# The last four attention units of a fused top-k attention and gated network take the path of all others

## The chip, the cores and the metric

The kernel runs on one core of one Trainium2 chip. The metric is the device time of one execution in microseconds, the median of three runs. Engines are called PE or TensorE (matmuls), DVE or VectorE, ACT or ScalarE, POOL or GpSimd, and SP or SyncE, whose queue here only issues DMAs.

## The reference, cut to what matters

Attention with 8 batches, 8 heads, 576 tokens and a head of 64 elements keeps the 32 largest scores of each row; its result, laid out as 4608 tokens by 512, goes through a network with a cosine gate.

```python
scores = scale * np.matmul(q, k.transpose(0, 1, 3, 2))
kth = np.partition(scores, -top_k, axis=-1)[..., -top_k:-top_k + 1]
scores = np.where(scores >= kth, scores, -1000000000.0)
scores = scores - np.max(scores, axis=-1, keepdims=True)
attn = np.exp(scores)
attn = attn / (np.sum(attn, axis=-1, keepdims=True) + 1e-09)
attn_out = np.matmul(attn, v)
x = attn_out.transpose(0, 2, 1, 3).reshape(B * S, H * D)      # 4608 x 512
h = x @ w_in                                                   # 4608 x 2048
out = (h * np.cos(h)) @ w_out                                  # 4608 x 512
```

## The kernel before, in words

**Units and blocks.** The 4608 tokens are cut into 36 blocks of 128. A *unit* is one block and one pair of heads, so there are 144 units, four per block (`NU` = 144). A block's network part starts when the attention of its four units has been written, transposed, into the tile `xT`.

**One unit of attention.** `scores` makes two 128 x 576 score matrices in PSUM (448 columns in a tile of tag `sc`, which has two buffers, the last 128 in the tile `rim`). `take_scores` copies them to `s` in SBUF on ScalarE. The search for the 32nd largest runs on VectorE in rounds of "eight largest" (MAX8) and "replace these" (MATCH_REPLACE8). A *folded* search works on 288 columns: `fold_high` makes the larger of the two halves of a row, `fold_sum` and `fold_low` on GpSimd the smaller (sum less larger, on the bits), four rounds search the larger, two the smaller, and `merge_first`, `merge_second` find the threshold in the two sorted lists. `bounds` and `distances` turn it into two biases, `mask` and `exponentials` (ScalarE) into weights with their sums, `sums` and `reciprocal` (VectorE) into 1/denominator.

**Two ways to transpose the weights.** Units 0 to 139 go through memory: `split` (GpSimd) separates the 16-bit halves of the weights and of the reciprocal into the tile `halves` (one buffer), `write_halves` writes them to memory, and `transposes` reads them back with a transposing DMA into `pT` (three buffers), both from SP's queue. `values` multiplies with v on TensorE, into `rim`, for two units at once; `take_values` multiplies by the transposed reciprocal on VectorE into `xT`. The last four units, 140 to 143, instead have `normalise` multiply the weights by the reciprocal on GpSimd, `transposes_now` transpose them as nine blocks of 128 x 128 on TensorE, into a tile of tag `sc` and `rim`, with three ScalarE copies to `pT`, and `values` and `take_values` (a ScalarE copy) follow in the same slot for that one unit. Units 142 and 143 are also searched without folding, on 576 columns.

**The network.** `ff1` is one call of the first product (two 128-column groups of h for one block; eight calls a block), `ff2` one of the second (two of 16 terms of the sum; eight calls a block). The first product's result lies in one of two PSUM banks (tag `mm`, also used by the second product's sum); `take_first` (ScalarE) evicts it twice, as h/2pi and as a rounded integer; `reduce_first` and `reduce_second` subtract them; `sines` (ScalarE) takes the cosine; `gate` multiplies; `ff2` reads that. `take_second` evicts the sum and sends it out. Reductions and gate run on GpSimd, and on VectorE once `ff["end"]` is set, as it is from slot 144 on.

**The order of the work.** The schedule is written out by hand: every engine runs its instructions in the order in which the program issues them. Slot `i` (`slot`) searches unit `i`, masks and takes exponentials of unit `i - 1`, sends unit `i - 2` to memory, and in even slots multiplies the pair `i - 4`, `i - 3` with v. `scored` says which slot makes which unit's scores; some slots make two. `feed(n)` puts up to `n` calls of `ff1` or `ff2` into TensorE's order, by credit (5 per slot less 0.9 per unit of scores), by `can_first` and `can_second` (are the inputs a few ticks old?) and by an alternation of two and two (`ff["kind"]`, `ff["half"]`). `open_bank` first evicts what is full when both banks are taken. Slots 141 to 144 are `last_slot`. A loop then forwards what is left of the network.

Of the launch, only the order of the slots matters here. The functions that the diff touches:

Of the kernel before, what the change touches and what calls it, by code (L numbers as in the profile page):

```python
# [10 lines left out]
F32 = mybir.dt.float32  # L11
# [6 lines left out]
P = 128  # L18
TOPK = 32
# [11 lines left out]
def kernel(  # L31
# [202 lines left out]
    def take_scores(u):  # L234
        s = u["s"] = work.tile([P, 2, S], F32, tag="s", name="s", bufs=4)
        nc.scalar.copy(out=s[:, :, 0:SB], in_=u["sc"][:, :, 0:SB])  # L236
        nc.scalar.copy(out=s[:, :, SB:S], in_=sc_ends[u["n"] % 2])  # L237
        if not u["folds"]:
            del u["sc"]

    def fold_high(u):

# [15 lines left out]

    def fold_sum(u):

        if not u["folds"]:
            return
        s = u["s"].bitcast(I32)
        u["low"] = work.tile([P, 2, HS], F32, tag="low", name="low", bufs=1)
        nc.gpsimd.tensor_tensor(  # L265
            out=u["low"].bitcast(I32), in0=s[:, :, 0:HS], in1=s[:, :, HS:S], op=ALU.add
        )

    def fold_low(u):

        if not u["folds"] or u["n"] in BUSY:
            return
        low = u["low"].bitcast(I32)
        nc.gpsimd.tensor_tensor(  # L274
            out=low, in0=low, in1=u["rest"][:, :, HS:S].bitcast(I32), op=ALU.subtract
        )
# [15 lines left out]
    def topk_first(u, w):  # L292

        u["top"] = tops[u["n"] % len(tops)]
        merges = w and w["folds"]
        if merges:
            merge_first(w)
        if u["folds"]:
            if u["n"] not in BUSY:
                fold_sum(u)  # L300
            fold_high(u)
        else:
            u["rest"] = work.tile([P, 2, S], F32, tag="rest", name="rest", bufs=1)
        if merges:
            merge_second(w)
        if u["folds"] and u["n"] in BUSY:
            fold_now(u)
        topk_round(u, 0, [lambda: bounds(w), lambda: distances(w)] if w else ())

    def topk_round(u, rnd, between=(), ahead=None):  # L310
        top, rest, lasts = u["top"], u["rest"], TOPK // 8 - 1
        end = TOPK - 1 - 8 * rnd
        at = top[:, :, end : end - 8 if rnd < lasts else None : -1, 0]
        if u["folds"]:
            search(
                at, rest[:, :, HS:S] if rnd == 0 else rest[:, :, 0:HS], rest[:, :, 0:HS], rnd < lasts,
                between if rnd < lasts else (),
            )
        else:
            search(at, u["s"] if rnd == 0 else rest, rest, rnd < lasts, between)  # L320
        if rnd < lasts:
            return
        del u["rest"]
        if u["folds"]:
            low = u.pop("low")
            for k in range(TOPK // 16):
                more = k < TOPK // 16 - 1
                if ahead and not more:
                    take_values(ahead)
                search(  # L330
                    top[:, :, 1 + 8 * k : 9 + 8 * k, 1], low, low, more,
                    () if more or rnd < lasts else between,
                )

# [22 lines left out]
    def bounds(u):  # L359

        top = u.pop("top").rearrange("p j r i -> p j (r i)")
        end = 2 * TOPK
        if not u["folds"]:
            nc.vector.tensor_copy(out=top[:, :, end - 1], in_=top[:, :, 0])
        less = u["less"] = top[:, :, end : end + 2]
        u["near"] = top[:, :, end - 1 : end + 1]
        nc.vector.tensor_reduce(
            out=less, in_=top[:, :, end - 2 : end].unsqueeze(3), axis=mybir.AxisListType.X,
            op=ALU.max, negate=True,
        )  # L370
# [35 lines left out]
    def both(u):  # L406
        return [lambda: sums(u), lambda: reciprocal(u)] if u else ()

    def normalise(u):
        s, rden = u["s"], u.pop("rden")  # L410
        for j in range(2):
            nc.gpsimd.tensor_scalar(
                out=s[:, j], in0=s[:, j], scalar1=rden[:, j : j + 1], scalar2=1.0,
                op0=ALU.mult, op1=ALU.mult,
            )

    def split(u):


# [14 lines left out]
    def transposes(u):  # L436
# [3 lines left out]
        nc.sync.dma_start_transpose(  # L440
            out=words.rearrange("p (c q) -> p c q", c=2 * NT + 2), in_=rows
        )

    def transposes_now(u):

        s = u.pop("s").rearrange("p j k -> p (j k)")
        tp = ps.tile([P, 2, 512], F32, tag="sc", name="tp", bufs=2)
        for c in range(2 * NT + 1):
            j, k = divmod(c, NT + 1)
            to = room[1][:, 0:P] if c == NT else tp[:, j, k * P : (k + 1) * P]  # L450
            nc.tensor.transpose(to, s[:, c * P : (c + 1) * P], ident)
        pT = u["pT"] = work.tile([P, 2 * NT + 2, P], F32, tag="pT", name="pT", bufs=3)
        for j in range(2):
            at = j * (NT + 1)
            nc.scalar.copy(
                out=pT[:, at : at + NT].rearrange("p c q -> p (c q)"), in_=tp[:, j]
            )
        nc.scalar.copy(out=pT[:, NT], in_=room[1][:, 0:P])

    def values(us):  # L460

# [17 lines left out]
    def take_values(us):  # L479
        blk, hp, n = block_of[us[0]["tok"]], us[0]["hp"], len(us)  # L480
        if "xT" not in blk:
            blk["xT"] = work.tile([P, NP, P], F32, tag="xT", name="xT", bufs=5)
        for i, u in enumerate(us):
            to, o, pT = blk["xT"][:, hp + i], room[0][:, i * P : (i + 1) * P], u.pop("pT")
            if u["paired"]:
                nc.vector.tensor_tensor(out=to, in0=o, in1=pT[:, 2 * NT + 1], op=ALU.mult)
            else:
                nc.scalar.copy(out=to, in_=o)
        blk["left"] -= n
        blk["tick"] = ff["tick"]  # L490

# [154 lines left out]
    def feed(n):  # L646

        ff["tick"] += 1
        while n > 0 and ff["credit"] >= 1:
            for kind in (ff["kind"], 1 - ff["kind"]):  # L650
                if (can_first, can_second)[kind]():
                    break
            else:
                return
# [14 lines left out]

    LAST = NU - NP
    scored, last, last_values = {}, {}, {}
    for i, u in enumerate(units):
        two = i % 2 == 0 and 2 < i < LAST + 2 and (len(u["parts"]) == 1 or u["hp"] == 0)
        scored.setdefault(i - 2 if two else i - 1, []).append(u)
        for part in u["parts"]:
            last[part[0], u["hp"]] = i - 2 if two else i - 1
            last_values[part[0], u["hp"]] = i
# [19 lines left out]

    for i, u in enumerate(units):  # L700
        u["n"] = i
        u["folds"] = i < LAST + 2
        u["paired"] = i < LAST

    def send(x):

# [4 lines left out]
    def slot(i, u, w, x, z):  # L711
# [37 lines left out]
        take_banks()  # L749
        if w and late:  # L750
            exponentials(w)
        take_scores(units[i + 1])
        if w and not late:
            exponentials(w)
        topk_round(u, 3, both(w), z)
# [8 lines left out]
        reduce_first()  # L764
        reduce_second()
        feed(1 if len(made) == 2 else 3)
        if i == LAST:
            sines(1)

    def last_slot(i, u, w, x, z):  # L770
        ff["late"] = False
        if u:
            topk_first(u, w)
            fold_low(u)
            topk_round(u, 1)
        else:
            bounds(w)
            distances(w)
        mask(w)
        exponentials(w)  # L780
        take_banks()
        sines(1)
        if z:
            values(z)
        if i + 1 < NU:
            scores(units[i + 1])
        if z:
            take_values(z)
        if i + 1 < NU:
            take_scores(units[i + 1])  # L790
        if x:
            send(x)
        if u:
            topk_round(u, 2, both(w))
            topk_round(u, 3)
        else:
            sums(w)
            reciprocal(w)
        normalise(w)
        gate(2)  # L800
        feed(2)
        transposes_now(w)
        take_banks()
        reduce_first()
        reduce_second()
        feed(1)
        values([w])
        take_values([w])
        feed(2)

    tt = ps.tile([P, 512], F32, tag="mm", name="warm", bufs=2)
    for _ in range(12):
# [4 lines left out]
    scores(units[0])  # L817
    take_scores(units[0])
    decode_first(3)
    for i in range(NU + 1):  # L820
        ff["end"] = i >= NU
        ff["credit"] = min(ff["credit"] + 5.0 - 0.9 * len(scored.get(i, [])), 5.3)
        ff["now"] += 1
        wq["ready"] = wq["done"]
        u, w = (units[i - n] if 0 <= i - n < NU else None for n in range(2))
        x = units[i - 2] if 0 <= i - 2 < LAST else None
        z = units[i - 4 : i - 2] if i % 2 == 0 and 0 <= i - 4 < LAST else None
        if i <= LAST:
            slot(i, u, w, x, z)
        else:  # L830
            last_slot(i, u, w, x, z)
    while first or second or full:
        ff["now"] += 1
        ff["credit"] = 2.0
        take_banks()
        gate(2)
        reduce_first()
        reduce_second()
        sines(1)
        gate(2)  # L840
        feed(2)


# [35 lines left out]
```

## Time and profile before

| What | us |
|---|---|
| median of three runs | 1461.11 |
| the three runs | 1461.11, 1459.79, 1464.31 |
| profiled execution, its own time | 1461.65 |
| profiled execution, span of the trace | 1459.9 |

| Engine | busy us | share of the span |
|---|---|---|
| TensorE, matmul | 1386.9 | 95% |
| VectorE | 1363.8 | 93% |
| GpSimd | 1157.5 | 79% |
| ScalarE | 1088.2 | 75% |

A line of the timeline gives the start, the busy time (neighbours of one form are merged), the engine, the line of the kernel, the operation, what it writes and reads with the shapes, and how many instructions. A bracket at the end is the idle time of the engine before it, and what ended it. Ends of matmuls are modelled, so the distance from one start to the next is the better measure of what they cost. Buffer numbers are left out of names. A span begins and ends with the traced instructions; the device time of the same execution is 1.75 us longer.

### The profile page before, as it was taken

How to read it: one execution, taken by the hardware profiler on the slowest of the kernel's cores; microseconds unless marked ns; L12 is line 12 of the kernel's file. 1: busy time of each engine (PE TensorE's matmuls, PEld its weight loads, DVE VectorE, ACT ScalarE, POOL GpSimd, SP SyncE). 2: the span in 40 equal slices, each digit the busy share in tenths (PEclk: the TensorE clock that was granted, in tenths of full speed). 3: DMA queues.
4: the chain of work that ended last, by engine and by line, in shares of the span. 5: the costliest groups of instructions: out<-in, count | busy, mean ns of one | idle time of the engine just before them, and what ended most of it. 6: DMA issues, size and time to landing. Idle time of an engine off the chain costs nothing.

```text
span 1459.9 us, 30230 instructions
## 1 busy us (share of the span) xinstructions
PE 1386.9 (95%) x10288; PEld 996.8 (68%) x10288; DVE 1363.8 (93%) x5213; ACT 1088.2 (75%) x1910; POOL 1157.5 (79%) x812
## 2 busy tenths in 40 slices
PE   4387899999999999999999999999999999999998
PEld 2265667777777767777777776777777777777665
DVE  7999999999999999999999999999999999999821
ACT  5787767877777777778777777777777787877641
POOL 5867878888888888888888887888888888888410
PEclk6598999999999999999999999999999999999999
DMA  8986687666665576657655666657665566655300
GB/s 254 282 235 192 175 183 182 155 161 190 179 159 152 168 180 169 161 144 201 185 168 143 144 180 182 170 149 185 192 169 144 152 171 168 166 152 152 62 8 15
DMA packets 427434, 240.00 MB, mean 164 GB/s; under 512 B 375952, under 2 KB 392592, under 8 KB 427280
## 3 DMA queue, kind: packets, MB, share of 16 engines
q1 hardware_dynamic: 418704, 216.88, 57.0%
q10 hardware_dynamic: 8576, 21.19, 4.1%
q8 instruction: 81, 1.33, 0.4%
q14 instruction: 73, 0.60, 0.1%
HBM read 45.09 MB, written 101.19 MB: 100 GB/s over the span
## 4 chain that ended last, share of the span: by engine, by line
PE 82%; DVE 8%; ACT 4%; DMA 3%; POOL 1%; issue 1%; SPq 1%; ACTq 0%; POOLq 0%
PE mm L537 31%; PE o L612 31%; PE rim L477 10%; PE sc L226 7%; DVE top L352 4%; DVE rest L357 2%; PE rim L226 2%; DMA v<-in_v_dram 1%; ACT s L391 1%; ACT s L383 1%; DMA k<-in_k_dram 1%; ACT L391 1%; DMA st<-in_moe_w_in_dram 1%; DVE rest L247 1%; DVE low L357 0%
## 5 line engine op out<-in xcount | busy, mean ns | idle before, releaser
L537 PEld LDWEIGHTS mm<-xT,w_in 128*128 128x128 f32 x4608 | 537.0, 192 | 74.8 <-issue 64.7
L612 PE MATMUL o<-w_out,g 128*128 128x512 f32 x1152 | 538.1, 600 | 12.0 <-POOL w_out L154 7.7
L537 PE MATMUL mm<-xT,w_in 128*128 128x128 f32 x4608 | 540.1, 275 | 6.8 <-ACT x L553 3.9
L352 DVE MAX8 top<-rest 128x8 f32<-128x288 f32 x1148 | 480.7, 454 | 0.0
L424 POOL COPY halves<-s 128x2304 uint16<-128x2304 uint16 x140 | 294.8, 2105 | 149.5 <-ACT s L391 149.1
L357 DVE MATCH_REPLACE8 rest<-top,rest 128x288 f32<-128x288 f32 (+1 forms) x860 | 377.0, 446 | 0.0
L612 PEld LDWEIGHTS o<-w_out,g 128*128 128x128 f32 x1152 | 202.4, 190 | 199.0 <-issue 184.2
L352 DVE MAX8 top<-low 128x8 f32<-128x288 f32 x568 | 240.0, 448 | 0.1
L391 ACT ACTIVATE s<-s,nd 128x576 f32<-128x576 f32 x288 | 220.2, 767 | 0.8
L383 ACT ACTIVATE s<-s,top 128x576 f32<-128x576 f32 x288 | 206.1, 766 | 0.0
L274 POOL TENSOR_TENSOR low<-low,rest 128x576 int32<-128x576 int32 x137 | 193.6, 1413 | 10.7
L265 POOL TENSOR_TENSOR low<-s 128x576 int32<-128x576 int32 x137 | 193.7, 1414 | 6.1 <-ACT s L237 4.9
L226 PE MATMUL sc<-k,q 64*128 64x448 f32 (+1 forms) x640 | 157.9, 591 | 36.8 <-DMA k<-in_k_dram 14.9
L551 ACT ACTIVATE g<-mm 128x512 f32<-128x512 f32 x144 | 85.8, 596 | 128.8 <-PE mm L537 124.6
L582 POOL TENSOR_TENSOR x<-g,x 128x1024 f32<-128x1024 f32 x68 | 160.9, 2366 | 5.7
L477 PE MATMUL rim<-pT,v 128*64 128x128 f32 (+1 forms) x2560 | 159.5, 269 | 2.8 <-DMA pT<-rows 2.8
L599 POOL TENSOR_TENSOR g<-g,x 128x1024 f32<-128x1024 f32 x68 | 161.0, 2367 | 1.3 <-ACT x L592 1.3
L477 PEld LDWEIGHTS rim<-pT,v 128*64 128x64 f32 x2560 | 132.8, 139 | 13.1 <-issue 4.0
L236 ACT COPY s<-sc 128x896 f32<-128x896 f32 x144 | 129.2, 897 | 3.9 <-PE sc L226 3.4
L237 ACT COPY s<-rim 128x256 f32<-128x256 f32 x144 | 55.1, 382 | 91.9 <-PE rim L477 91.9
L357 DVE MATCH_REPLACE8 low<-top,low 128x288 f32<-128x288 f32 x284 | 123.6, 443 | 0.0
L226 PEld LDWEIGHTS sc<-k,q 64*128 64x128 f32 (+1 forms) x640 | 47.5, 183 | 100.2 <-DVE rest L357 47.0
(59 smaller groups left out, 1335.8 us busy)
## 6 DMA issues: line engine op xcount, KB each, us to landing
rows<-halves SPq DMA_DIRECT2D x140, 640.0 KB, 3.0
out_dram<-ob ACTq DMA_DIRECT2D x36, 256.0 KB, 2.4
q<-in_q_dram SPq DMA_DIRECT2D x31, 288.0 KB, 3.9
v<-in_v_dram SPq DMA_DIRECT2D x32, 256.0 KB, 3.4
st<-in_moe_w_out_dram ACTq DMA_DIRECT2D x16, 512.0 KB, 5.1
st<-in_moe_w_in_dram SPq DMA_DIRECT2D x10, 512.0 KB, 6.9
k<-in_k_dram SPq DMA_DIRECT2D x31, 144.0 KB, 3.8
k<-in_k_dram SPq DMA_DIRECT2D x32, 128.0 KB, 3.8
```

Source lines behind the costliest of these rows:

```text
L226: nc.tensor.matmul(to[r0 : r0 + rows, j, 0 : k1 - k0], st["q"][d, q0 : q0 + rows], st["k"][d, k0:k1], start=True, stop=True,)
L265: nc.gpsimd.tensor_tensor(out=u["low"].bitcast(I32), in0=s[:, :, 0:HS], in1=s[:, :, HS:S], op=ALU.add)
L274: nc.gpsimd.tensor_tensor(out=low, in0=low, in1=u["rest"][:, :, HS:S].bitcast(I32), op=ALU.subtract)
L352: nc.vector.max(to[:, j], src[:, j])
L357: nc.vector.match_replace(rest[:, j], to[:, j], src[:, j], NEG)
L383: nc.scalar.activation(out=s[:, j], in_=s[:, j], func=AF.Prelu, bias=less[:, j, 1:2], scale=1.0, alpha=FAR)
L391: nc.scalar.activation(out=s[:, j], in_=s[:, j], func=AF.Exp, bias=nd[:, j : j + 1], scale=SCALE, accum_out=den[:, j, 0:1],)
L424: nc.gpsimd.tensor_copy(out=halves[:, :, 0 : 2 * S], in_=s.rearrange("p (k h) -> p h k", h=2))
L477: nc.tensor.matmul(o[d, to], lhsT, rhs, start=c == 0, stop=c == NT)
L537: nc.tensor.matmul(mm[:, at : at + w], w_in[f // FC][:, c, (f % FC) * P : (f % FC + 1) * P], blk["xT"][:, c], start=c == 0, stop=c == NC - 1,)
L599: eng.tensor_tensor(out=g, in0=g, in1=x, op=ALU.mult)
L612: nc.tensor.matmul(o, g[:, at : at + P], w_out[f], start=f == 0, stop=f == NF - 1)
```

## The change

The last four units go the way of all others. Every unit is searched folded; every unit goes through `split`, `write_halves` and `transposes`; `values` and `take_values` take them in pairs. `normalise` and `transposes_now` go, as do `last_slot` and all conditions on `u["folds"]` and `u["paired"]`. The ordinary `slot` runs for all 144 units. Three calls of the new function `drain` finish units 142 and 143: the first sends 142 to memory, masks 143 and multiplies the pair 140, 141 with v; the second sends 143; the third multiplies the pair 142, 143. `ff["end"]` is set ahead of the first. The network is moved on in each by `forward`, which is the body of the loop at the end made a function. Two rules of the planner change: unit 142's scores are made in slot 140 beside those of 141, and once `ff["end"]` is set and the second product of a block is about to begin, `feed` asks for a first product first.

```diff
-        if not u["folds"]:
-            del u["sc"]
...
-        merges = w and w["folds"]
-        if merges:
+        if w:
             merge_first(w)
-        if u["folds"]:
-            if u["n"] not in BUSY:
-                fold_sum(u)
-            fold_high(u)
-        else:
-            u["rest"] = work.tile([P, 2, S], F32, tag="rest", name="rest", bufs=1)
-        if merges:
+        if u["n"] not in BUSY:
+            fold_sum(u)
+        fold_high(u)
+        if w:
             merge_second(w)
...
-            if u["paired"]:
-                nc.vector.tensor_tensor(out=to, in0=o, in1=pT[:, 2 * NT + 1], op=ALU.mult)
-            else:
-                nc.scalar.copy(out=to, in_=o)
+            nc.vector.tensor_tensor(out=to, in0=o, in1=pT[:, 2 * NT + 1], op=ALU.mult)
...
-            for kind in (ff["kind"], 1 - ff["kind"]):
+            kinds = (ff["kind"], 1 - ff["kind"])
+            if ff["end"] and second and second[0][2] == 0:
+                kinds = (0, 1)
+            for kind in kinds:
...
-        two = i % 2 == 0 and 2 < i < LAST + 2 and (len(u["parts"]) == 1 or u["hp"] == 0)
+        two = i % 2 == 0 and 2 < i and (len(u["parts"]) == 1 or u["hp"] == 0)
...
-        take_scores(units[i + 1])
+        if i + 1 < NU:
+            take_scores(units[i + 1])
...
-        if i == LAST:
-            sines(1)
+    def forward(n):
+        ff["now"] += 1
+        ff["credit"] = n
+        take_banks()
+        gate(2)
+        reduce_first()
+        reduce_second()
+        sines(1)
+        gate(2)
+        feed(n)
+
+    def drain(w, x, z):
+        if x:
+            send(x)
+        if w:
+            merge_first(w)
+            merge_second(w)
+            bounds(w)
+            distances(w)
+            mask(w)
+            exponentials(w)
+            sums(w)
+            reciprocal(w)
+        forward(2)
+        if z:
+            values(z)
+            take_values(z)
+        forward(2)
...
-    for i in range(NU + 1):
-        ff["end"] = i >= NU
+    for i in range(NU):
...
-        u, w = (units[i - n] if 0 <= i - n < NU else None for n in range(2))
-        x = units[i - 2] if 0 <= i - 2 < LAST else None
-        z = units[i - 4 : i - 2] if i % 2 == 0 and 0 <= i - 4 < LAST else None
-        if i <= LAST:
-            slot(i, u, w, x, z)
-        else:
-            last_slot(i, u, w, x, z)
+        u, w, x = (units[i - n] if n <= i else None for n in range(3))
+        z = units[i - 4 : i - 2] if i % 2 == 0 and i >= 4 else None
+        slot(i, u, w, x, z)
+    ff["end"], ff["late"] = True, False
+    drain(units[NU - 1], units[NU - 2], units[NU - 4 : NU - 2])
+    drain(None, units[NU - 1], None)
+    drain(None, None, units[NU - 2 : NU])
     while first or second or full:
-        ff["now"] += 1
-        ff["credit"] = 2.0
-        take_banks()
-        gate(2)
-        reduce_first()
-        reduce_second()
-        sines(1)
-        gate(2)
-        feed(2)
+        forward(2)
```

More of the change, by code (lines that the diff above doesn't have):

```diff
@@ L259, in fold_sum @@
     def fold_sum(u):
-        if not u["folds"]:
-            return
         s = u["s"].bitcast(I32)
@@ L269, in fold_low @@
     def fold_low(u):
-        if not u["folds"] or u["n"] in BUSY:
+        if u["n"] in BUSY:
             return
@@ L294, in topk_first @@
         u["top"] = tops[u["n"] % len(tops)]
-        merges = w and w["folds"]
-        if merges:
+        if w:
             merge_first(w)
-        if u["folds"]:
-            if u["n"] not in BUSY:
-                fold_sum(u)
-            fold_high(u)
-        else:
-            u["rest"] = work.tile([P, 2, S], F32, tag="rest", name="rest", bufs=1)
-        if merges:
+        if u["n"] not in BUSY:
+            fold_sum(u)
+        fold_high(u)
+        if w:
             merge_second(w)
-        if u["folds"] and u["n"] in BUSY:
+        if u["n"] in BUSY:
             fold_now(u)
@@ L313, in topk_round @@
         at = top[:, :, end : end - 8 if rnd < lasts else None : -1, 0]
[L314 to L318, printed above, removed]
-        else:
-            search(at, u["s"] if rnd == 0 else rest, rest, rnd < lasts, between)
+        search(
+            at, rest[:, :, HS:S] if rnd == 0 else rest[:, :, 0:HS], rest[:, :, 0:HS], rnd < lasts,
+            between if rnd < lasts else (),
+        )
         if rnd < lasts:
@@ L323, in topk_round @@
         del u["rest"]
[L324 to L333, printed above, removed]
+        low = u.pop("low")
+        for k in range(TOPK // 16):
+            more = k < TOPK // 16 - 1
+            if ahead and not more:
+                take_values(ahead)
+            search(top[:, :, 1 + 8 * k : 9 + 8 * k, 1], low, low, more, () if more else between)
     def merge_first(u):
@@ L362, in bounds @@
         end = 2 * TOPK
-        if not u["folds"]:
-            nc.vector.tensor_copy(out=top[:, :, end - 1], in_=top[:, :, 0])
         less = u["less"] = top[:, :, end : end + 2]
@@ L407, in both @@
         return [lambda: sums(u), lambda: reciprocal(u)] if u else ()
[L409 to L415, printed above, removed]
     def split(u):
@@ L442, in transposes @@
         )
[L444 to L458, printed above, removed]
     def values(us):
@@ L663, in feed @@
             n, ff["credit"] = n - 1, ff["credit"] - 1
-    LAST = NU - NP
     scored, last, last_values = {}, {}, {}
     for i, u in enumerate(units):
-        two = i % 2 == 0 and 2 < i < LAST + 2 and (len(u["parts"]) == 1 or u["hp"] == 0)
+        two = i % 2 == 0 and 2 < i and (len(u["parts"]) == 1 or u["hp"] == 0)
         scored.setdefault(i - 2 if two else i - 1, []).append(u)
@@ L701 @@
         u["n"] = i
-        u["folds"] = i < LAST + 2
-        u["paired"] = i < LAST
     def send(x):
@@ L766, in slot @@
         feed(1 if len(made) == 2 else 3)
-        if i == LAST:
-            sines(1)
[L770 to L776, printed above, removed]
+    def forward(n):
[14 more added lines that the diff above has]
+            merge_second(w)
             bounds(w)
             distances(w)
-        mask(w)
-        exponentials(w)
-        take_banks()
-        sines(1)
+            mask(w)
[3 more added lines that the diff above has]
+        forward(2)
         if z:
             values(z)
-        if i + 1 < NU:
-            scores(units[i + 1])
-        if z:
             take_values(z)
[L789 to L799, printed above, removed]
-        gate(2)
-        feed(2)
-        transposes_now(w)
-        take_banks()
-        reduce_first()
-        reduce_second()
[L806 to L809, printed above, removed]
+        forward(2)
     tt = ps.tile([P, 512], F32, tag="mm", name="warm", bufs=2)
@@ L824 @@
         wq["ready"] = wq["done"]
-        u, w = (units[i - n] if 0 <= i - n < NU else None for n in range(2))
-        x = units[i - 2] if 0 <= i - 2 < LAST else None
-        z = units[i - 4 : i - 2] if i % 2 == 0 and 0 <= i - 4 < LAST else None
-        if i <= LAST:
-            slot(i, u, w, x, z)
-        else:
-            last_slot(i, u, w, x, z)
-    while first or second or full:
-        ff["now"] += 1
-        ff["credit"] = 2.0
-        take_banks()
-        gate(2)
[L837 to L841, printed above, removed]
+        u, w, x = (units[i - n] if n <= i else None for n in range(3))
[5 more added lines that the diff above has]
+    drain(None, None, units[NU - 2 : NU])
+    while first or second or full:
+        forward(2)
 _INS = ['q', 'k', 'v', 'moe_w_in', 'moe_w_out']
```

## The prediction

> **What bounds the kernel now.** I read the page's totals and slices, the comparison of stretches, TensorE's timeline from 1300 us on, its waits there, then the other engines at each wait. The stretches (columns: length, busy us of each engine, granted clock, DMA share, GB/s) come first:
>
> ```profile
> 1308.20:1326.90 18.70, 18.70 (x138) 13.57 (x137) 18.49 (x73) 14.78 (x26) 16.12 (x12) 1.00 0.59 151
> ...
> 1361.20:1399.00 37.80, 33.93 (x259) 24.58 (x257) 27.76 (x69) 26.80 (x50) 12.52 (x11) 1.00 0.16 43
> 1399.00:1459.90 60.90, 55.29 (x293) 37.24 (x293) 9.94 (x8) 16.26 (x25) 2.13 (x2) 1.00 0.04 14
> ```
>
> A steady pair of slots takes 18.70 us. TensorE has no gap in it and VectorE 0.2 us of gap. The last units' slots (third line) leave TensorE idle for 3.9 us, with every other engine slack too. So TensorE's ordered list of work sets the end: whatever takes matmuls or gaps out of it after slot 140 moves the end one for one. TensorE's timeline shows both:
>
> ```profile
> 1362.35 0.60 PE L451 MATMUL tp<-ident,s 128*128 128x128 f32 x4
> 1364.87 0.30 PE L451 MATMUL rim<-ident,s 128*128 128x128 f32 x1 [1.92 <-ACT s L237]
> 1365.00 0.60 PE L451 MATMUL tp<-ident,s 128*128 128x128 f32 x4
> ...
> 1388.87 0.66 PE L451 MATMUL tp<-ident,s 128*128 128x128 f32 x4 [1.69 <-POOL s L412]
> ...
> 1399.18 2.05 PE L537 MATMUL mm<-xT,w_in 128*128 128x128 f32 x16 [0.37 <-ACT x L553]
> ...
> 1413.66 3.70 PE L612 MATMUL o<-w_out,g 128*128 128x512 f32 x8 [1.22 <-DVE g L599]
> ...
> 1441.79 13.90 PE L612 MATMUL o<-w_out,g 128*128 128x512 f32 x32
> ```
>
> Nine transposes per unit stand in the list (L451), and the brackets are its only gaps: 1.92 + 1.69 + 0.37 + 1.22 = 5.2 us. The first two are waits of transposes (for ScalarE to leave the shared bank, and for GpSimd's normalising). The last matmul ends at 1455.69, and the last output takes 4.2 us more to the span's end at 1459.9.
>
> The path through memory, as unit 139 still takes it, on GpSimd and on SP's queue (SP's lines are issues):
>
> ```profile
> 1358.14 2.11 POOL L424 COPY halves<-s 128x2304 uint16<-128x2304 uint16 x1
> 1360.19 0.41 POOL L426 COPY halves<-rden 128x256 uint16<-128x256 uint16 x1
> ```
>
> ```profile
> 1360.62 0.34 SPq L434 DMA_DIRECT2D rows<-halves  x1
> 1363.62 3.10 SPq L440 DMA_TRANSPOSE pT<-rows  x1
> ```
>
> So 2.5 us of copies, 3.0 us until the transposing DMA is issued, then its landing: 5.0 us in the median, 7.2 at most, from the transfers' own summary.
>
> **The skill.** "TensorE: Matmul & The Clock Gate" (Step-by-step: what each phase is for) says that matmuls keep program order and only weight loads are pulled ahead. The trace agrees: at 1364.87 ready products stand 1.92 us behind one transpose. "VectorE: DVE Perf Modes" (The three transpose paths) gives 390 ns by TensorE and 1309 ns by DMA for one 128x128 bf16 block, TensorE being the quicker for latency; here nine f32 blocks cost about 1.0 us without their wait and twenty 16-bit blocks land in 5.0. "DMA: Bandwidth & Descriptors" (Anatomy of one DMA — SWDGE (gpsimd) path) says that DMA engines do not wait on semaphores, the issuing sequencer does. So on SP, unit 143's write stands behind unit 142's transposing issue. "ScalarE: Activation LUTs" (What ACT_TABLE_LOAD costs) states 1283 ns and a drain of 1380 per switch; the trace has the 1.28, but the exponential after the load at 1342.29 starts at 1343.59, so I charge 1.30.
>
> **The change, part by part.** I followed the planner's rules (credits, ticks, the two deques) through both versions. Until slot 140's scores the order is the same on every engine, so nothing before 1349.8 us moves.
>
> Removed: 4 x 9 transposes, which hold TensorE's list for 1.17, 0.98, 1.32 and 0.99 us apart from their gaps: 4.5 us. The gaps of 5.2 us go with the transposes and the old order. The four lone values steps break the first product into single calls: eight at 15.2 us in sum against 1.785 each in pairs (14.3), so 0.9 us of changeovers. The new order has three such singles, 0.3: a gain of 0.6. ScalarE's copies (L455, L458) and GpSimd's normalising (L412) cost nothing now, since neither is on the path.
>
> Added on VectorE: nothing of weight. Units 142 and 143 searched unfolded cost 8 maxima of 0.66 and 6 replacements of 0.73 (9.7 us); folded, a slot is 9.35. Each adds two GpSimd sums of 1.41, and four units add copies of 2.5 us. GpSimd has 16.1 busy of 18.7 in a steady pair, and these slots are such pairs. If that cover were gone, each unit's sums would hold its search by 2.8 us. ScalarE's table loads stay five from slot 141 on (in before at 1361.2, 1370.4, 1386.4, 1395.2, 1409.9; now two each in slots 141 and 143, one in the drain). SP gets four writes and four transposing issues more, 0.3 and 3 us of its queue each, past nothing: all loads are done, and the DMA share is 0.16 or less. Unit 139's write moves ahead by a few us.
>
> The list on TensorE, durations from the rows of before:
> - Slots 140 and 141 become an ordinary pair: second product at 1346.83, end 1365.5.
> - Slot 142: second product 1.8, scores of 143 1.2, values of 138 and 139 2.3, two second calls 3.5, one first call; slot 143: one first, one second, one first, two second. End 1385.1. The gate of group (33, second half) must be done by 1381.6. On GpSimd: reduction ends 1372.7 (an ordinary slot, 37.4 us after 1335.36), copies of 141 2.5, two sums 2.8, gate 2.4: 1380.3. Slack 1.3.
> - First drain step: one first call, to 1387.0. The next needs a PSUM bank. One holds block 33's output and the other is emptied by ScalarE only after the exponentials of 143. VectorE's slot 143 starts at 1373.9 (slot 141 began at 1355.19, a pair takes 18.70) and ends at 1383.2, bounds at 1384.1, masks and exponentials 2.96 (1357.09 to 1360.05 in before), eviction 1.15: 1388.2. **A new wait of 1.3 us.** Queued behind it are the first call, the values of 140 and 141 and all later products. Then one first call, values, two second calls: 1396.0.
> - Second step: three first calls and one second. ScalarE: output eviction 1396.05, table load and sine done 3.44 later as at 1408.91, so 1399.5, gate on VectorE 1400.8; the second product wants it at 1401.4. Slack 0.6.
> - Third step: two second calls, to 1406.7, then values of 142 and 143. Unit 143's trip: exponentials done 1387.1; copies from 1387.7 (the single halves buffer is free when 142's write has landed) to 1390.2; write issued 1390.8, behind 142's transposing issue; transposing issue 1393.8, after its buffer comes free at 1393; landed 1398.8, at worst 1401. TensorE asks at 1406.7: hidden, 8 us to spare. Uncovered, the trip from the exponentials on is 11.7 us.
> - After that: values to 1409.0, one second 1410.8, block 35's products 3.6, 3.5, 3.6, 3.5, 7.1, and the unbroken last eight second calls 13.9: 1446.0. The last gates (1428, 1437) come 2 us or more before they are asked for.
>
> The end is 1446.0 + 4.2 = 1450.2, or 9.7 us less. By parts: 4.5 + 5.2 + 0.6 - 1.3 = 9.0. They differ by roundings at the changeovers; I take 9.5. On the profiled execution's own 1461.65 that gives 1452.2; the median of the runs, 1461.11, lies 0.5 lower, so **1451.6 us**. Unknown is the new wait: bounded by 0 (bank early) and by 1.3 plus a slot's stretch of some 5 us. I take 1.3.
>
> **Rivals.**
> 1. The chain of gates is late: both thin slacks (1.3 and 0.6) are overrun when the sines or GpSimd run 2.5 us behind. For: GpSimd's sums and copies stand ahead of the gate in slot 143. Against: that order ran on time in every steady slot. Cost (2.5 - 1.3) + (2.5 - 0.6) = 3.1: 1454.7.
> 2. VectorE becomes the bound of the last two slots: bounds of 143 come 6 us late, and the bank behind its exponentials holds TensorE by 7.3 instead of 1.3. Gain 3.5, 1457.6: no difference. For: VectorE is 99% full in steady slots. Against: the unfolded slots of before were no shorter.
> 3. The memory trip of the last pair is exposed. Nothing else may run on TensorE past it: the values of 142 and 143 stand in order, and VectorE's gate of block 34 stands behind their eviction. It needs 143's data 8 us late to bite and 8 + 9.5 + 4.4 = 21.9 us late, landing after 1420, to end slower. With 24 us late: 1461.1 - 9.5 + 16 = 1467.6. For: the trip is the longest latency here and SP's queue is serial. Against: the worst landing seen is 2.2 us over the median, and DMA is nearly silent then (share 0.01).
> 4. The change doesn't do what it says: excluded, the transposes leave the list.
>
> **Chances.** A difference of 0.3%, 4.4 us, is about what a measurement of this kernel tells from none. Forecast, gain 7 to 11.5: 0.58. Rival 1, gain 4.4 to 7: 0.20. Rival 2, within 4.4 either way: 0.14. Rival 3: 0.08. So faster 0.78, same 0.14, slower 0.08. The range goes from no new wait and a little noise (1448.8) up into rival 2, to 1458; the likeliest case alone spans 1449.6 to 1454.
>
> **What would show it.** No TensorE transposes after the warm-up; the page's TensorE count down by 36, one per transpose (10288 to 10252); ordinary slots to 1383; one gap of 1 to 2 us at the first drain step behind ScalarE's eviction (L553 of before); no gap before the last values; last matmul near 1446. A gap before the values of 142 that names the DMA, a gap before a second product that names a gate in slot 143 or step two, or an end of the search past 1388, would be rivals 3, 1 and 2.

## The result and the profile after

| | before | changed |
|---|---|---|
| median | 1461.62 us (4 runs, 1459.79 to 1464.31) | 1448.09 us (4 runs, 1446.51 to 1448.69) |
| profiled execution, its own time | 1461.65 us | 1448.69 us |
| span of that profile | 1459.9 us | 1446.9 us |

The ratio is 0.9904, with a 95% interval of 0.9886 to 0.9922: 13.5 us less where 9.5 were forecast. The median is 0.7 us below the lower end of the range, 1448.8. The direction, and nearly all of the mechanism, are as forecast. What the range had no room for is found below.

TensorE's timeline of the changed kernel (start, busy time, engine, line, operation, names, count; in brackets the idle time ahead and what ended it) answers to the one shown of before, where slot 140's second product stood at

```profile
1346.83 1.88 PE L612 MATMUL o<-w_out,g 128*128 128x512 f32 x4
```

In the changed kernel:

```profile
1344.23 1.88 PE L566 MATMUL o<-w_out,g 128*128 128x512 f32 x4
...
1378.86 3.60 PE L566 MATMUL o<-w_out,g 128*128 128x512 f32 x8
1382.29 1.95 PE L491 MATMUL mm<-xT,w_in 128*128 128x128 f32 x16
1385.51 2.05 PE L491 MATMUL mm<-xT,w_in 128*128 128x128 f32 x16 [1.27 <-ACT x L507]
1387.49 1.09 PE L434 MATMUL rim<-pT,v 128*64 128x128 f32 x16
...
1403.96 1.09 PE L434 MATMUL rim<-pT,v 128*64 128x128 f32 x16
...
1429.27 13.90 PE L566 MATMUL o<-w_out,g 128*128 128x512 f32 x32
```

There is one bracket from slot 140 to the end, the wait of 1.27 us for the PSUM bank in the first drain step (forecast 1.3), behind ScalarE's eviction. The values of the last pair (1403.96) wait for nothing. The stretch from the start of slot 140's second product to the end of the last matmul, called the **tail** from here on, took 1429.27 + 13.90 - 1344.23 = 98.94 us, against 1455.69 - 1346.83 = 108.86 before: 9.92 less, where the list gave 9.7.

The path through memory of unit 143, on GpSimd and on SP's queue of the changed kernel:

```profile
1385.29 2.11 POOL L397 COPY halves<-s 128x2304 uint16<-128x2304 uint16 x1 [3.11 <-DMA rows<-halves]
1387.34 0.40 POOL L399 COPY halves<-rden 128x256 uint16<-128x256 uint16 x1
```

```profile
1385.22 3.12 SPq L413 DMA_TRANSPOSE pT<-rows  x1
1388.38 0.57 SPq L407 DMA_DIRECT2D rows<-halves  x1
1393.34 3.40 SPq L413 DMA_TRANSPOSE pT<-rows  x1
```

The copies wait for the single halves buffer (3.11 us), as worked out. The copies end at 1387.74, but the write is issued only at 1388.38, when unit 142's transposing issue has ended (1385.22 + 3.12): it stood behind it on SP's queue, as the prediction had it. The write then took 4.96 us to its transposing issue instead of 3.0, with unit 142's transposing transfer in flight, and the transposing transfer took 6.4 us to land: 1399.7. TensorE asks at 1404.0. Of the 8 us to spare 4.2 were there by this count (a run below makes it 5.4).

Which terms made the 9.92? From one start to the next in TensorE's timelines, less the brackets, summed over the tail:

| us in the tail | before | changed | difference |
|---|---|---|---|
| transposes | 4.46 | 0 | 4.46 |
| idle | 5.20 | 1.27 | 3.93 |
| first product | 36.85 | 36.06 | 0.79 |
| second product | 49.20 | 48.95 | 0.25 |
| values | 9.63 | 9.34 | 0.29 |
| scores | 3.52 | 3.32 | 0.20 |

The last four lines are the same work. They are shorter by 1.53 us while the list changes from one kind of product to another less often (27 times instead of 38, transposes counted); the prediction counted 0.6 for it, from the first product alone.

The two spans differ by 13.0 us. That leaves 13.0 - 9.9 = 3.1 us. Of it 0.5 lies after the last matmul (4.2 us before, 3.7 after) and 2.6 lies ahead of slot 140, where no instruction had changed. That stretch, from the span's start to slot 140's second product, is called the **head**.

### The profile page after: what moved, and what is told of

The parts are those of the page before. It is cut to its first block, busy times and chain, and to the rows that moved or that the text cites. A ratio compares the mean times of both kernels' runs of the same rounds, so it can differ in the third digit from the quotient of the medians.

```text
span 1446.9 us, 30176 instructions
## 1 busy us (share of the span) xinstructions
PE 1380.3 (95%) x10252; PEld 992.2 (69%) x10252; DVE 1359.4 (94%) x5237; ACT 1082.6 (75%) x1894; POOL 1166.0 (81%) x816
## 4 chain that ended last, share of the span: by engine, by line
PE 87%; DVE 7%; ACT 3%; DMA 2%; SPq 1%; POOL 0%; issue 0%; ACTq 0%
PE mm L491 33%; PE o L566 33%; PE rim L434 11%; PE sc L226 8%; DVE top L337 3%; PE rim L226 2%; DVE rest L342 2%; DMA v<-in_v_dram 1%; DMA st<-in_moe_w_in_dram 1%; DVE rest L245 1%; ACT s L366 0%; ACT s L374 0%; DVE low L342 0%; DVE w_out L144 0%; DMA k<-in_k_dram 0%
## 5 line engine op out<-in xcount | busy, mean ns | idle before, releaser
L397 POOL COPY halves<-s 128x2304 uint16<-128x2304 uint16 x144 | 303.2, 2105 | 156.4 <-ACT s L374 153.3
L342 DVE MATCH_REPLACE8 rest<-top,rest 128x288 f32<-128x288 f32 x864 | 376.5, 443 | 0.0
L337 DVE MAX8 top<-low 128x8 f32<-128x288 f32 x576 | 243.6, 449 | 0.1
L270 POOL TENSOR_TENSOR low<-low,rest 128x576 int32<-128x576 int32 x139 | 196.5, 1414 | 10.9
```

The source lines that it names most:

```text
L270: nc.gpsimd.tensor_tensor(out=low, in0=low, in1=u["rest"][:, :, HS:S].bitcast(I32), op=ALU.subtract)
L337: nc.vector.max(to[:, j], src[:, j])
L342: nc.vector.match_replace(rest[:, j], to[:, j], src[:, j], NEG)
L397: nc.gpsimd.tensor_copy(out=halves[:, :, 0 : 2 * S], in_=s.rearrange("p (k h) -> p h k", h=2))
```

## Experiments

Each kernel is the changed one with one edit, unless it says otherwise. The tail is read from each one's TensorE timeline.

### Is the head's 2.6 us the change's?

The unchanged pair, once more each, and the changed kernel a third time. No edit.

> The changed kernel again, nothing edited. Measure: the tail, from the start of slot 140's lone second product to the end of the last matmul, 98.9 us in the first profile of the changed kernel and 108.9 in that of the kernel before. The program up to slot 140 is the same, yet slot 140's fold began 2.6 us earlier (1343.3 against 1345.9). Chance theory: that head is a draw of transfers' arrival in the first slots and at slot 54, so this profile's fold of slot 140 falls anywhere between 1341 and 1347, and the tail is again 98.9 within 0.3. Layout theory: the smaller program shifts the head for good, so it is 1343.3 within 0.3.

> The kernel before again, nothing edited. Tail 108.9 within 0.3 in both theories. Chance theory: the fold of slot 140 begins anywhere between 1341 and 1347. Layout theory: at 1345.9 within 0.3, apart from every profile of a changed kernel.

> The changed kernel a third time. Ten profiles so far have slot 140's fold beginning anywhere from 1342.7 to 1346.1, of changed kernels and of kernels before alike. Chance theory: the median over many executions is 9.9 us under the kernel before, ratio 0.9932 (0.992 to 0.9945), and the first measurement's 0.9904 was 3 us of luck in the head. Layout theory: 0.9904 again.

| | first profile | again | a third time |
|---|---|---|---|
| changed: tail, us | 98.94 | 98.94 | 98.94 |
| changed: slot 140's second product starts at | 1344.23 | 1343.62 | 1350.33 |
| changed: ratio (95% interval) | 0.9904 (0.9886 to 0.9922) | 0.9935 (0.9918 to 0.9951) | 0.9927 (0.9901 to 0.9952) |
| before: tail, us | 108.86 | 108.85 | |
| before: slot 140's second product starts at | 1346.83 | 1345.40 | |
| before: ratio (95% interval) | | 0.9998 (0.9988 to 1.0008) | |

The layout theory falls: the head of the changed kernel's third profile is longer than either of before. The chance theory stands, and its own band for the head was too narrow (slot 140's fold began at 1349.44 in the third profile, where 1347 was the upper end). Over the fourteen profiles of this study, changed and not, slot 140's second product starts anywhere from 1343.58 to 1350.33. Where that comes from is visible in VectorE's timelines, by the start of each slot's fold. Slots 56 to 90 take 317.91 to 317.93 us in all fourteen. Slot 5 begins at 59.1 to 62.2. Slots 5 to 54 take 472.6 to 477.3, most of that spread in slot 8 alone (12.0 to 15.9), and slots 54 to 56, where a new batch's keys and queries are first used, 20.1 to 21.4. Slots 18, 90 and 126, also at changes of batch, spread by 0.5 to 0.8 us each. Outside these places the slots up to 140 repeat within 0.1 us, but for half a microsecond in one profile.

In slot 8 it is no input that is late but a transposing transfer: it took 11.6 us to land in the changed kernel's first profile and 14.8 in its third, against a median of 5.0. TensorE's timelines, first profile, then third:

```profile
97.84 0.91 PE L434 MATMUL rim<-pT,v 128*64 128x128 f32 x6 [3.25 <-DMA pT<-rows]
103.06 1.34 PE L434 MATMUL rim<-pT,v 128*64 128x128 f32 x10 [7.27 <-DMA pT<-rows]
```

At slot 54 TensorE's timeline of before shows a short wait for keys, part of the 1.1 us by which the first profiles of the two kernels part there; the changed kernel's first profile doesn't have it:

```profile
539.48 1.25 PE L226 MATMUL sc<-k,q 64*64 64x448 f32 x3 [0.17 <-DMA k<-in_k_dram]
```

So the head is a draw, renewed at each execution, of when transfers arrive; what delays the one in slot 8 was not tried. All eighteen runs of the changed kernel in the three measurements have a median of 1449.85 us, the fifty-nine runs of before beside them 1461.11: 11.3 us, of which the tail and the end explain 10.4.

The 0.5 us after the last matmul repeat (3.7 us in each of the three profiles, against 4.2 in both of before). They are not the output's: it lands 2.67 us after the last matmul in the changed kernel and 2.68 before. The difference lies behind that, among the closing instructions of the program, those of SyncE above all; why they take less time was not tried.

### The transposes without their waits

```diff
     def drain(w, x, z):
...
         forward(2)
+        tp = ps.tile([P, 2, 512], F32, tag="sc", name="tp", bufs=2)
+        for c in range(12):
+            nc.tensor.transpose(tp[:, c % 2, 0:P], ident, ident)
         if z:
```

> The changed kernel with 36 further TensorE transposes of the identity, twelve in each drain step after its first forward, into a free PSUM tile that nobody reads: the removed transposes without their waits. List theory: 36 x 0.11 = 4.0 us and three changeovers of 0.1: tail 98.9 + 4.2 = 103.1 (102.7 to 103.6). Rival (transposes are cheap beside matmuls, only their waits cost): below 100.

Tail 102.87, 3.93 more: 0.109 us for each transpose. The rival falls; the nine transposes of a unit cost TensorE's list about a microsecond even where nothing waits. The bracket of 1.27 stood unchanged. Ratio to before 0.9954 (0.9933 to 0.9976).

### One part alone: the folded search in the kernel before

```diff
-        u["folds"] = i < LAST + 2
+        u["folds"] = True
...
         else:
+            merge_first(w)
+            merge_second(w)
             bounds(w)
```

> The kernel before with one part of the change alone: units 142 and 143 are searched folded. Transposes by TensorE and the old order stay. List theory: the search of the last two is not on TensorE's list, only its waits for the normalised weights (1.7 us) may shrink: tail 108.9 - 1 (107 to 109). Rival (the folded search brings the gain): 105 or less.

Tail 106.65, 2.21 less than before's 108.86, a little more than expected: 1.69 of it is the wait for GpSimd's normalising, which is gone, as the transposes of unit 142 now find the weights ready. In this kernel's TensorE timeline:

```profile
1363.11 0.30 PE L451 MATMUL rim<-ident,s 128*128 128x128 f32 x1 [1.91 <-ACT s L237]
...
1385.26 0.60 PE L451 MATMUL tp<-ident,s 128*128 128x128 f32 x4
```

The folded search accounts for about a fifth of the tail's gain, mostly through that wait; not for the rest. Ratio 0.998 (0.9967 to 0.9993).

### The other way round: the last two units unfolded in the changed kernel

```diff
-        if w:
+        merges = w and w["n"] < NU - 2
+        if merges:
             merge_first(w)
-        if u["n"] not in BUSY:
-            fold_sum(u)
-        fold_high(u)
-        if w:
+        if u["n"] < NU - 2:
+            if u["n"] not in BUSY:
+                fold_sum(u)
+            fold_high(u)
+        else:
+            u["rest"] = work.tile([P, 2, S], F32, tag="rest", name="rest", bufs=1)
+        if merges:
             merge_second(w)
...
+        if u["n"] >= NU - 2:
+            search(at, u["s"] if rnd == 0 else rest, rest, rnd < lasts, between)
...
```

> The changed kernel with units 142 and 143 searched unfolded. VectorE's part of each of these slots grows from 9.35 us to some 10.5 to 11, so unit 143's exponentials come about 3 us later, and ScalarE empties the PSUM bank behind them: the wait of 1.27 us in the first drain step becomes about 4. List theory with the bank behind the exponentials: tail 98.9 + 2.8 (101 to 102.5). Rival (the wait of 1.27 is only the bank's own eviction, the search is off the path by more than 3 us): 98.9 to 99.3.

Tail 103.94, 5.0 more: past the expected band. The waits are where they were expected and as long (TensorE's timeline of this kernel):

```profile
1381.39 2.05 PE L506 MATMUL mm<-xT,w_in 128*128 128x128 f32 x16 [1.04 <-ACT x L522]
...
1391.89 3.41 PE L506 MATMUL mm<-xT,w_in 128*128 128x128 f32 x16 [3.23 <-ACT x L522]
```

That is 1.04 + 3.23 - 1.27 = 3.0 more. But the first call behind the long wait takes 3.41 us instead of 2.05, and the stretches say why (length, busy us of TensorE, weight loads, VectorE, ScalarE, GpSimd, then the granted clock, DMA share, GB/s; the granted clock is the share of TensorE's full clock):

```profile
1386.00:1388.50 2.50, 2.50 (x19) 1.99 (x17) 1.63 (x7) 0.77 (x2) 0.90 (x2) 1.00 0.00 0
1388.50:1391.80 3.30, 0.16 (x2) 0.00 (x0) 0.32 (x2) 3.30 (x8) 0.90 (x1) 0.93 0.49 199
1391.80:1395.20 3.40, 3.31 (x16) 3.22 (x16) 0.00 (x0) 0.04 (x1) 1.55 (x2) 0.56 1.09 214
```

The clock fell to half 0.5 us before the wait ended and stayed there for 3.4 us. That call's 1.4 us are the clock's; some 0.6 us more lie in other calls and were not traced. So a late search reaches TensorE through the bank behind the exponentials, as the prediction had it, and costs more than its wait. Ratio 0.9956 (0.9946 to 0.9965).

### How late may the last pair's data be?

```diff
         write_halves(x)
+        for _ in range(3 if x["n"] == NU - 1 else 0):
+            rows = dram.tile([P, 2, 2 * S + P], U16, tag="rows", name="rows")
+            nc.sync.dma_start(out=rows, in_=x["rows"])
+            x["rows"] = rows
         transposes(x)
```

The same with 2 and with 1 for the 3.

> The changed kernel with unit 143's rows copied three times more from memory to memory before the transposing transfer, each waiting for the one ahead: about 3 x 4 = 12 us later (9 to 15). In the profile of the changed kernel that transfer lands at 1399.7 and TensorE asks for it at 1404.0, so 4.2 us are spare. List theory: the tail grows by the delay less 4.2, some 8 us (5 to 11), as one gap ahead of the last pair's values, to about 106.7. Rival (the trip is hidden by more than that, for other products can go first): growth below 2.

> The changed kernel with unit 143's rows copied twice more from memory to memory instead of three times. With three copies TensorE waited 6.21 us, and its clock was at 0.50 for some 4 us after that; the tail was 107.4, 8.45 us longer. One copy less is some 4.5 us less: a wait of 1.7. Clock theory (what a wait costs beyond itself is the halved clock after a long one): the clock stays at 1.00 and the tail grows by the wait alone, 98.9 + 1.7 = 100.6 (99.5 to 101.7). Rival (each late microsecond costs 8.45/6.21 = 1.36 whatever its length, through traffic or order): 98.9 + 2.3 = 101.2, more than the wait that is shown by a third.

> The changed kernel with unit 143's rows copied once more from memory to memory. Two copies gave a wait of 2.29 us, each copy takes some 4.5 us, so here the transposing transfer lands about 2 us before TensorE asks: no wait, the clock at 1.00 throughout, tail 98.9 to 99.2. Rival (the slack was less than 4.5 us, and the two-copy run's wait was cut short by faster copies): a wait of up to 1 us and a tail of up to 100.

| copies | wait ahead of unit 143's values, us | tail, us | longer by |
|---|---|---|---|
| 0 | none | 98.94 | |
| 1 | none | 98.94 | 0 |
| 2 | 2.29 | 103.15 | 4.21 |
| 3 | 6.21 | 107.39 | 8.45 |

The ratios to before are 0.9939 (0.9916 to 0.9961), 0.9952 (0.9936 to 0.9967) and 0.9987 (0.9976 to 0.9997) for one, two and three copies.

Counted from the start of the tail, the last transposing transfer is issued at 49.1, 54.0, 58.2 and 62.4 us and lands at 55.5, 59.6, 63.3 and 67.2. One copy costs nothing: the trip is hidden with room. With two and three copies the wait comes ahead of unit 143's values alone, at 60.9 us, since those of 142 go first. So the unedited trip has 60.9 - 55.5 = 5.4 us to spare, 1.2 more than the 4.2 that were counted. Both theories written for two copies fall: the wait grew the tail by nearly twice its length (4.21 for 2.29), and the ratio is not that of three copies (8.45 for 6.21). What is common is an extra of 1.9 and 2.2 us. The wait in the kernel with two copies, and its stretches, show it:

```profile
1411.48 1.09 PE L434 MATMUL rim<-pT,v 128*64 128x128 f32 x16 [2.29 <-DMA pT<-rows]
```

```profile
1409.00:1411.40 2.40, 0.19 (x4) 0.00 (x0) 0.00 (x0) 0.00 (x0) 0.00 (x0) 1.00 0.91 206
1411.40:1412.70 1.30, 1.22 (x20) 1.07 (x20) 0.00 (x0) 0.00 (x0) 0.00 (x0) 1.00 0.00 0
1412.70:1413.70 1.00, 1.00 (x4) 0.46 (x3) 0.86 (x3) 0.00 (x0) 0.00 (x0) 0.56 0.06 16
1413.70:1414.70 1.00, 1.00 (x3) 0.48 (x2) 0.76 (x1) 0.00 (x0) 0.00 (x0) 0.50 0.00 0
1414.70:1415.70 1.00, 1.00 (x3) 0.48 (x2) 0.00 (x0) 0.00 (x0) 0.00 (x0) 0.50 0.00 0
```

The wait of 2.29 us ended at 1411.48, and the clock fell to 0.50 only at 1412.8, with TensorE at work again, for 3.4 us. So it was the clock, as the clock theory said, but its idea that a short wait is spared was wrong at 2.29 us. The kernel before had waits of 1.92 and 1.69 us with the clock at 1.00 throughout. What tells these apart is worked out at the end.

### The planner's rule undone

```diff
-            if ff["end"] and second and second[0][2] == 0:
-                kinds = (0, 1)
```

> The changed kernel without the planner's rule that a first product goes ahead of a block's opening second product. List theory: block 34's opening second call follows one pair of first calls and waits for the gate, about 1.4 us; and block 35's last first calls come later, so only 3.4 us of second calls cover the 5.0 us chain eviction, reduction, sine, gate: 1.6 us more. Tail 98.9 + 3.0 = 101.9. Rival (the rule is idle, the gain is the transposes' alone): 98.9.

Tail 102.56, 3.6 more. The two new waits are those expected, ahead of block 34's opening second call and in block 35, both for a gate on VectorE:

```profile
1397.75 3.67 PE L566 MATMUL o<-w_out,g 128*128 128x512 f32 x8 [1.31 <-DVE g L553]
...
1439.01 7.13 PE L566 MATMUL o<-w_out,g 128*128 128x512 f32 x16 [1.60 <-DVE g L553]
```

The other 0.7 us come with four more changes of kind (31 instead of 27). Without this small rule more than a third of the tail's gain is lost. The prediction worked with the rule in its order of calls, but gave it no price of its own. Ratio 0.9956 (0.9942 to 0.9969).

### A version that does without the wait of 1.27 us

```diff
-        forward(2)
+        forward(1 if w and z else 2)
         if z:
             values(z)
             take_values(z)
-        forward(2)
+        forward(3 if w and z else 2)
```

> The changed kernel with the values of units 140 and 141 put between the two first calls of the first drain step, one call ahead of them and three after. List theory: the 1.27 us wait for the PSUM bank is covered by 2.3 us of values, nothing else moves: tail 98.9 - 1.2 = 97.7. Rival (the wait only moves, to the gate before block 34's second product, whose slack was 0.6 us by the prediction): tail 98.3 to 98.9.

> The version with the values between the first calls again, beside the changed kernel on the same chip. Tail 97.4 as before, 1.5 us shorter than the changed kernel's; the median lies 1.5 us below its median, if the head's scatter of some 3 us averages out.

Tail 97.41 both times, and no bracket at all in TensorE's timeline of it: the bank is emptied while the values of units 140 and 141 run. Ratio to before 0.9926 (0.9913 to 0.9938), then 0.9914 (0.9889 to 0.9939). Its medians were 1449.71 beside the changed kernel's 1450.86, and 1447.99 beside 1450.52: it is the quicker of the two by 1.2 and 2.5 us, around the 1.53 us of its tail. The intervals of the two kernels' ratios overlap, so the tail shows this gain and the whole time does not. The wait didn't move.

## Why the prediction was wrong, and where it was right

- **TensorE's list sets the end: right.** The order of calls was as worked out, the tail 98.94 us where the list had 1446.0 - 1346.83 = 99.2, and it repeats to 0.01 us.
- **Removed transposes, 4.5: right** (4.46; 3.93 where as many were put back, in three groups, without any wait).
- **The gaps, 5.2 less a new wait of 1.3: right** (5.20 and 1.27), with its place, its releaser and its dependence on unit 143's exponentials.
- **Changeovers, 0.6: undersized;** 1.53. Counted were the first product's lone calls; values, scores and second products gain too.
- **VectorE and GpSimd unchanged in the last slots: right.** The last search ended 36.0 us into the tail; forecast were 36.4.
- **The trip through memory hidden with 8 us to spare: right that it is hidden, off in size.** 5.4 us were left: the write took 5.0 instead of 3.0 and the transposing landing 6.4 instead of 5.0. Unit 142's transfer was in flight beside the write. Block 33's output was in flight for 5.1 us beside the transposing transfer; in the runs with one, two and three copies, where that transfer comes later and clear of the output or nearly so, it took 5.6, 5.0 and 4.9. That points to neighbours in flight, but neither was tried by itself. The "7.2 at most" was the longest landing of the last stretch only; the whole profile of before has one of 8.8.
- **"Nothing before 1349.8 us moves", and from it the range: the step that failed.** No instruction there moved, but its time isn't fixed. The end was worked out on the head of the one profile there was, slot 140's second product at 1346.83. The lower end, 1448.8, is 1451.6 less the 1.3 of the new wait and 1.5 for "a little noise", where fourteen profiles put that product anywhere from 1343.58 to 1350.33, a spread of 6.75 us. The first measurement of the changed kernel drew short heads: if tail and end took the same 102.6 us in each of its four runs, their spans of 1444.7 to 1446.9 put slot 140's second product at about 1342 to 1344 (an estimate), where the middle of the fourteen profiles is 1345.6. Two more measurements gave 0.9935 and 0.9927; the forecast, 1451.6 on 1461.11, is 0.9935.
- **The 4.2 us after the last matmul:** 3.7, in the three profiles of the changed kernel. Missed; it lies behind the output's landing, in the program's closing instructions.
- **The rivals.** 1 (late gates) and 2 (a late search) did not happen; the run with the unfolded search shows rival 2's path at work with a smaller delay. Rival 1 lay near: the gate of the slack of 0.6 us ended 0.45 us ahead of the product that reads it (1397.03 + 1.23 on VectorE, 1398.71 on TensorE). Rival 3 was priced one for one with the lateness. The runs with two and three copies show the wait and 1.9 to 2.2 us of slow clock with it.

## What to carry to other kernels

Where one engine's ordered list sets the end, write out the list with durations from the trace and look for the brackets: here that gave the tail within 0.3 us, and the one bracket left pointed to a reordering worth 1.5 us more. But a forecast of a whole run needs the scatter of the parts that don't change, and that takes several profiles of one kernel, not one; compare the changed stretch by itself first. Work that was put into a wait for a bank cost nothing here (97.41 us against 98.94). A wait of TensorE can cost more than its length: those of 2.29, 3.23 and 6.21 us brought 1.4 to 2.2 us of slow clock on top.

## What was unexpected of the hardware

- After waits of 2.29, 3.23 and 6.21 us TensorE's granted clock was 0.50 for some 3 to 4 us, at an extra cost of 1.4 to 2.2 us; after waits up to 1.92 us in the tails it stayed at 1.00. In the first case the fall came 1.3 us after work had resumed. "TensorE: Matmul & The Clock Gate" (Part 1: The HAM clock gate) tells of a free-running window of about 3.4 us and of a halved clock after one idle window. The half, the late fall and the window agree with it, but a wholly idle window was not needed. In the clock records of all fourteen profiles every change lies on a grid of 3.41 us. Summing TensorE's idle time (waits over 0.1 us) in each step of that grid, from the first fall to the last matmul, gives one rule without exception in these runs: the clock fell from 1.00 after the 38 steps that were idle for 0.554 or more, and stayed at 1.00 after the 5543 steps that were idle for 0.551 or less. The wait of 2.29 us filled 0.61 of one step. The 1.92 us of before were split over two, 0.36 and 0.20. So the place of a wait on the grid counts as well as its length. From these numbers, as an estimate, a wait under 0.55 x 3.41 = 1.9 us that stands alone is safe, and one of twice that is safe nowhere.
- Thirty-four slots (56 to 90) took 317.91 to 317.93 us in fourteen profiles, while the first fifty-four spread over 6.3 us. An execution's scatter sits in the first slots, in slot 8 behind one transposing transfer that can be slow to land (11.6 and 14.8 us in the two profiles compared), and at changes of batch.
